# Attention inside a fused kernel: how the row sums are inverted and spread, and where the row maxima stand in VectorE's queue

## The chip, the cores and the metric

The kernel runs on one NeuronCore of a Trainium2 chip. The metric is the device time of one execution in microseconds (us); lower is better. PE is TensorE, DVE is VectorE, ACT is ScalarE, POOL is GpSimd and SP is the queue that issues the DMAs.

## The reference

```python
def _attn_ref(q, k, v):                      # 2 x 8 heads, 576 tokens, head dimension 64
    q_rot, k_rot = (rotate(q), rotate(k))    # rotary embedding
    scores = scale * np.matmul(q_rot, k_rot.transpose(0, 1, 3, 2))
    scores = scores - np.max(scores, axis=-1, keepdims=True)
    attn = np.exp(scores)
    attn = attn / (np.sum(attn, axis=-1, keepdims=True) + 1e-09)
    return np.matmul(attn, v).astype(np.float32)

def reference(**kwargs):
    attn_out = _attn_ref(**attn_kwargs)
    B, H, S, D = attn_out.shape
    x = np.ascontiguousarray(attn_out.transpose(0, 2, 1, 3)).reshape(B * S, H * D)
    x = _moe_ref(x=x, **moe_kwargs)          # x @ w_in, ELU, @ w_out (512 -> 2048 -> 512)
    return _moe2_ref(x=x, **moe2_kwargs)     # x @ w_in, Mish, @ w_out
```

## The kernel before

The kernel has two parts. Attention comes first, and behind it two feed-forward layers (ELU, then Mish). The change touches attention alone.

Attention works on pairs of heads, `NP` = 8 of them. A pair has nine tiles of 128 query rows: eight whole ones, and one that holds the last 64 rows of both heads (index 8). A tile is a step `u` of the loop in `attention()`; `i` is its index in the pair (`TPP` = 9) and `p` the pair. In a step the following instructions go to the engines' queues, each queue being worked off in the order in which it is written (`tc.manual_schedule()` leaves the order as it is in the program):

- `prepare`: GpSimd rotates the next but one pair (`rope_part`) and splits the next pair into high and low parts (`split_half`); SP issues the DMAs that stack these parts.
- `do_S(u)`: TensorE writes the scores of tile u to PSUM, in four matmuls of 288 columns (six for index 8). There are two score buffers, so `do_S(u)` needs the one that `do_exp(u - 2)` has read.
- `do_x`: VectorE multiplies a finished output group in `psA` by the inverse sums in `R`.
- `do_T(u - 3)` (`LAG` = 3): TensorE transposes the exponentials of the tile three steps back, into `psT` and `psL`.
- `do_inverse`, at i = 4 for the first four tiles of the pair (group g = 0) and at i = 0 of the next pair for the other five (g = 1): VectorE adds 1e-9 to the sums, takes the reciprocal, and copies each value 64 times into `rw` (for g = 1 it also multiplies a mask by the fifth column). Its first instruction waits for the sum that the exp of the step before leaves.
- `do_keep`: ScalarE copies the spread inverse sums from `psA` to `R`.
- `do_spread` and `do_av`, at the steps named in `plan`: TensorE turns the columns of `rw` into rows (a matmul with the identity), or multiplies the transposed exponentials `pt` with v, head by head, into 64 partitions of `psA` each. Spreads stand at i = 6 and i = 2, products with v at i = 7, 0, 3 and 5.
- `do_evac(u - 3)`: the transposed tile goes from `psT` to `pt`, on VectorE for the indices in `ON_DVE`, otherwise on ScalarE. `do_evac_last`, at three steps of a pair, takes `psL`, always on VectorE.
- `do_max(u)`: VectorE takes the extreme of each row of the scores (a minimum, since q was scaled by a negative number).
- `do_exp(u)`: ScalarE takes the exponential with that extreme as its bias, and leaves the row sum (`accum_out`).
- `do_xh` and `do_xl`, in the step after a group's last product: ScalarE rounds the output to its high part `XH`, and GpSimd subtracts that for the low part `XL` (VectorE in the last three pairs).
- From step 49 on, parts of the preparation of the first eight weight tiles (`weight_part`): one instruction on GpSimd, three on VectorE, one on ScalarE, one on GpSimd.

So the order on VectorE in a step was `do_x`, `do_inverse`, `do_evac`, `do_evac_last`, `do_max`; and the loop that sets the order of the work is do_S(u), do_max(u), do_exp(u), do_S(u + 2).

Of the kernel before, what the change touches and what calls it, by code (L numbers as in the profile page):

```python
# [10 lines left out]
F32 = mybir.dt.float32  # L11
F32R = mybir.dt.float32r
I32 = mybir.dt.int32
AF = mybir.ActivationFunctionType
ALU = mybir.AluOpType
AX = mybir.AxisListType
# [11 lines left out]
def kernel(  # L28
# [11 lines left out]
    nc = tc.nc  # L40
    NP = qk.shape[0]
# [12 lines left out]
    TPP = 9  # L54
    NU = NP * TPP
# [174 lines left out]
    def attention(att, ps, tail):  # L230
        idn = att.tile([128, 128], F32, name="idn")
        tab = att.tile([128, 4, S], F32, name="tab")
        idn2 = att.tile([128, 64], F32, name="idn2")
        half_mask = att.tile([128, 16], F32, name="half_mask")
        psT = [ps.tile([128, 4, 128], F32, name=f"psT{k}") for k in range(2)]
        psL = ps.tile([128, 4, 128], F32, name="psL")
        psA = ps.tile([128, 512], F32, name="psA")
# [97 lines left out]
        mn_t = {}  # L335
        sm_t = {}
        rc_t = {}
        R_t = {}
        ON_DVE = (0, 2, 4, 6)

        def do_S(u):
            p, i = divmod(u, TPP)
# [32 lines left out]
        def do_max(u):  # L375
            m = att.tile([128, 16], F32, tag="mn", name="mn", bufs=4)[:, 0:1]
            nc.vector.tensor_reduce(out=m, in_=psS[u][:, :, :HS], axis=AX.XY, op=ALU.min)  # L377
            mn_t[u] = m

        def do_exp(u):  # L380
            P = att.tile([128, S], F32, tag="P", name="P", bufs=PB)
            p, i = divmod(u, TPP)
            g, j = (0, i) if i < 4 else (1, i - 4)
            if j == 0:
                sm_t[p, g] = att.tile([128, 16], F32, tag="sm", name="sm", bufs=3)
            nc.scalar.activation(  # L386
                out=P.rearrange("p (j n) -> p j n", j=2), in_=psS.pop(u)[:, :, :HS],
                func=AF.Exp, scale=-1.0, bias=mn_t.pop(u), accum_out=sm_t[p, g][:, j:j + 1],
            )
            P_t[u] = P  # L390

        def do_inverse(p, g):
            n = 4 + g
            r = att.tile([128, 16], F32, tag="rc", name="rc", bufs=2)
            nc.vector.tensor_scalar(
                out=r[:, :n], in0=sm_t.pop((p, g))[:, :n], scalar1=1e-9, scalar2=None, op0=ALU.add
            )
            nc.vector.reciprocal(out=r[:, :n], in_=r[:, :n])
            w = att.tile([128, 3, 2, 64], F32, tag="rw", name="rw", bufs=1)
            nc.vector.tensor_copy(  # L400
                out=w[:, 0:2], in_=r[:, 0:4].rearrange("p (h t) -> p t h", h=2).unsqueeze(3).to_broadcast([128, 2, 2, 64])
            )
            if g:
                nc.vector.tensor_scalar(
                    out=w[:, 2], in0=half_mask[:, 0:2].unsqueeze(2).to_broadcast([128, 2, 64]),
                    scalar1=r[:, 4:5], scalar2=None, op0=ALU.mult,
                )
            rc_t[p, g] = w

        def do_spread(p, g):  # L410
            w = rc_t.pop((p, g))
            for t in range(2 + g):
                nc.tensor.matmul(
                    psA[:, 128 * t:min(128 * t + 128, 256 + 64 * g)],
                    lhsT=w[:, t].rearrange("p h d -> p (h d)"), rhs=idn if t < 2 else idn2,
                    start=True, stop=True,
                )

        def do_keep(p, g):
# [56 lines left out]
        def do_x(p, g):  # L476
            x = R_t[p, g]
            nc.vector.tensor_tensor(out=x, in0=psA[:, :(256, 320)[g]], in1=x, op=ALU.mult)
# [5 lines left out]
        def do_xl(p, g, eng):  # L484
            x, hi, lo = x_parts(p, g)
            eng.tensor_tensor(out=lo, in0=x, in1=plain(hi), op=ALU.subtract)
# [11 lines left out]
                pair.append(t)  # L498
            bd.append(pair)
        qb = [att.tile([128, 2, S], F32R, name=f"qb{i}") for i in range(2)]  # L500
        for r in range(2):
            rows = slice(64 * r, 64 * r + 64)
            nc.vector.memset(half_mask[rows, 0:1], 1.0 - r)
            nc.vector.memset(half_mask[rows, 1:2], float(r))
        split_alloc(0)
        def keep_warm(n):
            for _ in range(n):
# [40 lines left out]
        ends, spreads = {}, {}  # L548
# [6 lines left out]
        for u in range(max(av_at) + 2):  # L555
            p, i = divmod(u, TPP)
            for k in range(8):
                if i == (k if p else min(k + 2, 8)) and p + 1 < NP:
                    prepare(p + 1, k)
            if i == 8 and p + 1 < NP:  # L560
                load_v(p + 1)
            if p == NP - 3 and i == 1:
                open_job()
                open_job()
            if p == NP - 4 and i == 4:
                prefetch_weights(3)
            if u < NU:
                do_S(u)
            if u < LAG + 4:
                keep_warm(FILL[u])  # L570
            for (pp, g) in ends.get(u - 1, []):
                do_x(pp, g)
            if 0 <= u - LAG < NU:
                do_T(u - LAG)
            if i == 4 and u < NU:
                do_inverse(p, 0)
            if i == 0 and u:
                do_inverse(p - 1, 1)
            for (pp, g) in spreads.get(u - 1, []):
                do_keep(pp, g)  # L580
            for (pp, g, c) in av_at.get(u, []):
                if g == "r":
                    do_spread(pp, c)
                else:
                    do_av(pp, g, c)
            if u >= NU:
                tail(u - NU, False)
            if 0 <= u - LAG < NU:
                do_evac(u - LAG)
                if (u - LAG) % TPP in (3, 7, 8):  # L590
                    do_evac_last((u - LAG) % TPP)
            if u < NU:
                do_max(u)
                do_exp(u)
            if u == 0:
                for t in pt_t:
                    nc.vector.memset(t[S - 512:128, :, 4, :], 0.0)
                nc.vector.tensor_tensor(out=idn2, in0=idn[:, 0:64], in1=idn[:, 64:128], op=ALU.add)
            if u in (0, 2):
                nc.vector.memset(plain(qb[1 - u // 2][64:128]), 0.0)  # L600
            if u == 1:
                rope_half(1, 2, nc.vector)
                first_hi(*HEAD[-1])
                first_lo(*HEAD[-1])
                stack_q(0)
            for (pp, g) in ends.get(u - 1, []):
                do_xh(pp, g)
                do_xl(pp, g, nc.gpsimd if u < (NP - 3) * TPP else nc.vector)
            for _ in range(PARTS[u % 2] if u >= (NP - 3) * TPP + 4 else 0):
                if njob[0] < 2 * GF:  # L610
                    weight_part()
            if u >= NU:
                tmp_pool[0] = att
                tail(u - NU, True)
                tmp_pool[0] = None
# [262 lines left out]
```

## Time and profile before

| what | value |
|---|---|
| device time, median of 3 runs | 647.3 us (644.89 to 649.81) |
| the profiled execution | 651.54 us, its span 649.0 us |
| TensorE busy | 588.4 us (91%) |
| VectorE busy | 441.9 us (68%) |
| ScalarE busy | 354.8 us (55%) |
| GpSimd busy | 240.8 us (37%) |
| mean granted TensorE clock | 0.955 |

Attention takes the first third of the span: the first row maximum starts at 12.5 us, the last at 213.8 us. The pairs begin (by the maximum of their first tile) at 12.5, 43.0, 67.6, 89.7, 114.3, 138.8, 163.9 and 191.4 us. A share of busy time over the whole span mixes this part with the feed-forward part, so the views are read by stretches. A timeline row gives start, length, engine, line, instruction and tiles, and in brackets the idle time of the engine just before it with what ended that.

### The profile page before, as it was taken

To read this page: it belongs to the slowest core of one execution; us is meant where nothing else is said; L and a number is where in the kernel's file an instruction comes from. 1 tells how busy PE (TensorE), PEld (TensorE's weight loads), DVE (VectorE), ACT (ScalarE), POOL (GpSimd) and SP (SyncE) were. 2 spreads that over 40 slices of the span, in tenths; PEclk is the share of its full clock that TensorE was granted. 3 is DMA by queue.
4 is the path that set the end of the run, shared out by engine and by line. 5 is a ranking of instruction groups with operands and counts; after the bars stand their busy time and mean duration, and the time that the engine had idled before them with its cause. 6 is when DMAs were issued, how large, how long until landed. Compare 5 with 4: busy or idle time off the path is not lost.

```text
span 649.0 us, 10299 instructions
## 1 busy us (share of the span) xinstructions
PE 588.4 (91%) x3874; PEld 525.1 (81%) x3874; DVE 441.9 (68%) x679; ACT 354.8 (55%) x621; POOL 240.8 (37%) x218
## 2 busy tenths in 40 slices
PE   7888878778686879999999999999699999999997
PEld 6766656656454759999999999999489989989986
DVE  6656756666877247667777777879767966965552
ACT  2334444445345346665545455578477686485670
POOL 6576566482522102323232323244624524324000
PEclk9779989888799879999999999999989999999999
DMA  6572553751342101223222222313414223210022
GB/s 202 148 213 101 125 155 124 220 131 43 112 125 84 34 1 66 98 66 98 68 96 83 81 84 79 97 67 106 137 46 135 82 83 129 82 34 17 17 65 97
DMA packets 43921, 62.17 MB, mean 96 GB/s; under 512 B 13920, under 2 KB 32096, under 8 KB 43104
## 3 DMA queue, kind: packets, MB, share of 16 engines
q1 hardware_dynamic: 43872, 61.52, 31.3%
q8 instruction: 30, 0.49, 0.3%
q14 instruction: 19, 0.16, 0.1%
HBM read 46.20 MB, written 2.36 MB: 75 GB/s over the span
## 4 chain that ended last, share of the span: by engine, by line
PE 40%; issue 30%; DVE 13%; POOL 12%; ACT 5%; DMA 1%; SPq 0%; POOLq 0%; ACTq 0%; DVEq 0%
PE ps_h L709 15%; PE ps_s L183 12%; PE ps_s L370 5%; PE psA L463 4%; DVE mn L377 3%; POOL wu L96 3%; ACT P L386 3%; PE psT L431 3%; POOL wi1l L123 3%; POOL wo0l L123 2%; POOL wo1l L123 2%; POOL wi0l L123 2%; DVE wu L104 1%; DVE pt L445 1%; DVE rw L400 1%
## 5 line engine op out<-in xcount | busy, mean ns | idle before, releaser
L386 ACT ACTIVATE P<-ps_s,mn 128x576 f32<-128x576 f32 x72 | 53.3, 741 | 86.2 <-DVE mn L377 83.1
L463 PE MATMUL psA<-pt,v_t 128*64 128x256 f32 (+1 forms) x320 | 50.5, 450 | 22.5 <-ACT R L422 22.4
L377 DVE TENSOR_REDUCE mn<-ps_s 128x1 f32<-128x576 f32 x72 | 53.6, 745 | 17.0 <-PE ps_s L370 16.9
L123 POOL TENSOR_TENSOR wi1l<-wu,wi1h 128x512 fp32r<-128x512 f32 x16 | 25.3, 1579 | 101.6 <-ACT wi1h L122 101.6
L183 PE MATMUL ps_s<-XH,wi1h 128*128 128x288 f32 x256 | 54.5, 294 | 1.5 <-ACT tb L637 1.5
L183 PE MATMUL ps_s<-XH,wi0h 128*128 128x288 f32 x256 | 55.1, 297 | 0.8 <-DVE tb L218 0.7
L463 PEld LDWEIGHTS psA<-pt,v_t 128*64 128x64 f32 x320 | 21.6, 146 | 41.2 <-ACT R L422 25.9
L183 PE MATMUL ps_s<-XL,wi1h 128*128 128x288 f32 x256 | 54.7, 295 | 0.0
L183 PE MATMUL ps_s<-XL,wi0h 128*128 128x288 f32 x256 | 54.7, 295 | 0.0
L183 PE MATMUL ps_s<-XH,wi0l 128*128 128x288 f32 x256 | 54.5, 294 | 0.0
L183 PE MATMUL ps_s<-XH,wi1l 128*128 128x288 f32 x256 | 54.4, 293 | 0.0
L100 DVE TENSOR_SCALAR wu<-wu 128x512 int32<-128x512 int32 x64 | 31.3, 489 | 33.4 <-POOL wu L96 33.4
L104 DVE SCALAR_TENSOR_TENSOR wu<-raw,wu 128x512 int32<-128x512 int32 x64 | 49.6, 775 | 1.9
L370 PE MATMUL ps_s<-ka,qa 128*128 128x288 f32 x112 | 31.5, 365 | 20.1 <-ACT P L386 20.1
L108 DVE SCALAR_TENSOR_TENSOR wu<-raw,wu 128x512 int32<-128x512 int32 x64 | 48.0, 751 | 1.7
L123 POOL TENSOR_TENSOR wo0l<-wu,wo0h 128x512 fp32r<-128x512 f32 x16 | 25.3, 1583 | 64.2 <-ACT wo0h L122 60.7
L96 POOL TENSOR_SCALAR wu<-raw 128x512 f32<-128x512 f32 x64 | 47.2, 737 | 5.3
L431 PE MATMUL psT<-idn,P 128*128 128x128 f32 x288 | 47.9, 293 | 0.0
L123 POOL TENSOR_TENSOR wo1l<-wu,wo1h 128x512 fp32r<-128x512 f32 x16 | 24.2, 1515 | 62.1 <-ACT wo1h L122 62.1
L123 POOL TENSOR_TENSOR wi0l<-wu,wi0h 128x512 fp32r<-128x512 f32 x16 | 22.6, 1414 | 65.4 <-ACT wi0h L122 55.9
L217 DVE SCALAR_TENSOR_TENSOR tb<-ta,tb 128x576 f32<-128x576 f32 x30 | 22.7, 758 | 35.3 <-ACT tb L216 35.2
L370 PEld LDWEIGHTS ps_s<-ka,qa 128*128 128x128 f32 x112 | 18.3, 206 | 33.7 <-ACT P L386 25.3
(149 smaller groups left out, 1631.9 us busy)
## 6 DMA issues: line engine op xcount, KB each, us to landing
raw<-in_w_in_dram SPq DMA_DIRECT2D x32, 512.0 KB, 3.7
raw<-in_w_out_dram SPq DMA_DIRECT2D x32, 512.0 KB, 3.2
qk_t<-in_qk_dram SPq DMA_DIRECT2D x6, 1152.0 KB, 5.5
qa<-qh SPq DMA_DIRECT2D x28, 144.0 KB, 2.6
v_t<-in_vp_dram SPq DMA_DIRECT2D x8, 320.0 KB, 3.0
out_dram<-Y SPq DMA_DIRECT2D x9, 256.0 KB, 2.0
ka<-kh SPq DMA_DIRECT2D x14, 144.0 KB, 2.5
ka<-kl SPq DMA_DIRECT2D x14, 144.0 KB, 2.8
```

What stands on the lines that cost most here:

```text
L96: nc.gpsimd.tensor_scalar(out=u, in0=high.bitcast(F32), scalar1=REBASE, scalar2=0.0, op0=ALU.mult, op1=ALU.add)
L100: nc.vector.tensor_scalar(out=ui, in0=ui, scalar1=3, scalar2=0x7FFFFFF8, op0=ALU.logical_shift_left, op1=ALU.bitwise_and)
L104: nc.vector.scalar_tensor_tensor(out=ui, in0=high, scalar=-0x80000000, in1=ui, op0=ALU.bitwise_and, op1=ALU.bitwise_or)
L108: nc.vector.scalar_tensor_tensor(out=ui, in0=low, scalar=29, in1=ui, op0=ALU.logical_shift_right, op1=ALU.bitwise_or)
L123: nc.gpsimd.tensor_tensor(out=lo, in0=u, in1=plain(hi), op=ALU.subtract)
L183: nc.tensor.matmul(o[:, j, :HS], lhsT=w[:, cc, :], rhs=x[:, b, cc, j * HS:j * HS + HS], start=(k == 0), stop=(k == 3 * NC - 1),)
L370: nc.tensor.matmul(o[:, j, :HS], lhsT=l, rhs=r(slice(j * HS, j * HS + HS)), start=(a == 0), stop=(a == n - 1),)
L377: nc.vector.tensor_reduce(out=m, in_=psS[u][:, :, :HS], axis=AX.XY, op=ALU.min)
L386: nc.scalar.activation(out=P.rearrange("p (j n) -> p j n", j=2), in_=psS.pop(u)[:, :, :HS], func=AF.Exp, scale=-1.0, bias=mn_t.pop(u), acc ...
L431: nc.tensor.transpose(tv[:, c, :], P[:, c * 128:c * 128 + 128], idn)
L463: nc.tensor.matmul(o[64 * h:64 * h + 64, :n], lhsT=v_t[p][:, c, 64 * h:64 * h + 64], rhs=pt_t[g][:, h, c, :], start=(c == 0), stop=(c == 4),)
L709: nc.tensor.matmul(o, lhsT=l, rhs=w, start=(k == 0), stop=(k == 3 * GF - 1))
```

## The change

- The sums of a group go to every second element of one of three lasting tiles (`sums`), whose other elements are set to 1e-9 once. `do_inverse` adds the two elements of each pair (a reduction) and takes the reciprocal. The copy into `rw`, the mask and its multiplication are gone, and so are `half_mask` and `idn2`.
- `do_spread` takes the single column of inverse sums as stationary operand with a stride of zero, 64 times, for 64 partitions of `psA` at a time: four matmuls for g = 0 and six for g = 1, where there were two and three of 128 partitions.
- `do_max(u)` stands right behind `do_x`, ahead of `do_inverse` and of both evacuations.
- The evacuation of index 8 goes to VectorE and that of index 6 to ScalarE.
- `do_xh` and `do_xl` come one step later while the loop has score tiles left, and `do_xl` is on GpSimd for all pairs but the last.

```diff
@@ def attention
-        idn2 = att.tile([128, 64], F32, name="idn2")
-        half_mask = att.tile([128, 16], F32, name="half_mask")
+        sums = [att.tile([128, 8, 2], F32, name=f"sums{k}") for k in range(3)]
...
-        ON_DVE = (0, 2, 4, 6)
+        ON_DVE = (0, 2, 4, 8)
...
@@ def do_exp
-            if j == 0:
-                sm_t[p, g] = att.tile([128, 16], F32, tag="sm", name="sm", bufs=3)
+            sm_t[p, g] = sums[(2 * p + g) % 3]
             nc.scalar.activation(
                 out=P.rearrange("p (j n) -> p j n", j=2), in_=psS.pop(u)[:, :, :HS],
-                func=AF.Exp, scale=-1.0, bias=mn_t.pop(u), accum_out=sm_t[p, g][:, j:j + 1],
+                func=AF.Exp, scale=-1.0, bias=mn_t.pop(u), accum_out=sm_t[p, g][:, j, 0:1],
             )
@@ def do_inverse
             r = att.tile([128, 16], F32, tag="rc", name="rc", bufs=2)
-            nc.vector.tensor_scalar(
-                out=r[:, :n], in0=sm_t.pop((p, g))[:, :n], scalar1=1e-9, scalar2=None, op0=ALU.add
-            )
+            nc.vector.tensor_reduce(out=r[:, :n], in_=sm_t.pop((p, g))[:, :n, :], axis=AX.X, op=ALU.add)
             nc.vector.reciprocal(out=r[:, :n], in_=r[:, :n])
-            w = att.tile([128, 3, 2, 64], F32, tag="rw", name="rw", bufs=1)
-            nc.vector.tensor_copy(
-                out=w[:, 0:2], in_=r[:, 0:4].rearrange("p (h t) -> p t h", h=2).unsqueeze(3).to_broadcast([128, 2, 2, 64])
-            )
-            if g:
-                nc.vector.tensor_scalar(
-                    out=w[:, 2], in0=half_mask[:, 0:2].unsqueeze(2).to_broadcast([128, 2, 64]),
-                    scalar1=r[:, 4:5], scalar2=None, op0=ALU.mult,
-                )
-            rc_t[p, g] = w
+            rc_t[p, g] = r
@@ def do_spread
-            w = rc_t.pop((p, g))
-            for t in range(2 + g):
+            r = rc_t.pop((p, g))
+            for j in range(4):
+                h, t = divmod(j, 2)
                 nc.tensor.matmul(
-                    psA[:, 128 * t:min(128 * t + 128, 256 + 64 * g)],
-                    lhsT=w[:, t].rearrange("p h d -> p (h d)"), rhs=idn if t < 2 else idn2,
-                    start=True, stop=True,
+                    psA[64 * h:64 * h + 64, 128 * t:128 * t + 128],
+                    lhsT=r[:, j:j + 1].to_broadcast([128, 64]), rhs=idn, start=True, stop=True,
                 )
+            for h in range(2 * g):
+                nc.tensor.matmul(
+                    psA[64 * h:64 * h + 64, 256:320],
+                    lhsT=r[:, 4:5].to_broadcast([128, 64]), rhs=idn[:, 64 * h:64 * h + 64], start=True, stop=True,
+                )
@@ set-up
-        for r in range(2):
-            rows = slice(64 * r, 64 * r + 64)
-            nc.vector.memset(half_mask[rows, 0:1], 1.0 - r)
-            nc.vector.memset(half_mask[rows, 1:2], float(r))
+        for t in sums:
+            nc.vector.memset(t[:, :, 1:2], 1e-9)
@@ the loop over steps
             for (pp, g) in ends.get(u - 1, []):
                 do_x(pp, g)
+            if u < NU:
+                do_max(u)
             if 0 <= u - LAG < NU:
                 do_T(u - LAG)
...
             if u < NU:
-                do_max(u)
                 do_exp(u)
             if u == 0:
                 for t in pt_t:
                     nc.vector.memset(t[S - 512:128, :, 4, :], 0.0)
-                nc.vector.tensor_tensor(out=idn2, in0=idn[:, 0:64], in1=idn[:, 64:128], op=ALU.add)
...
-            for (pp, g) in ends.get(u - 1, []):
+            for (pp, g) in ends.get(u - (1 if u >= NU else 2), []):
                 do_xh(pp, g)
-                do_xl(pp, g, nc.gpsimd if u < (NP - 3) * TPP else nc.vector)
+                do_xl(pp, g, nc.gpsimd if pp < NP - 1 else nc.vector)
```

## Rows read from the trace of the kernel before

**Rows 1.** The page, part 2: granted TensorE clock, in tenths, in 40 slices
```profile
PEclk9779989888799879999999999999989999999999
```

**Rows 2.** Busy time by stretch; columns: stretch, length, engines, clock, DMA share, GB/s
```profile
12.00:43.00 31.00, 27.48 (x139) 21.73 (x139) 20.50 (x31) 9.74 (x24) 22.06 (x19) 0.72 0.59 162
...
67.60:89.70 22.10, 17.74 (x133) 13.61 (x133) 15.10 (x26) 11.40 (x27) 14.07 (x12) 1.00 0.49 139
89.70:114.30 24.60, 19.46 (x133) 15.15 (x133) 16.20 (x27) 11.39 (x27) 14.00 (x12) 0.93 0.43 122
...
138.80:163.90 25.10, 20.29 (x131) 16.23 (x132) 18.55 (x34) 12.45 (x29) 13.48 (x12) 0.86 0.33 89
163.90:191.40 27.50, 20.36 (x133) 14.75 (x132) 20.82 (x39) 12.64 (x30) 10.42 (x11) 0.88 0.45 126
191.40:213.80 22.40, 15.48 (x105) 11.49 (x104) 16.22 (x30) 11.65 (x27) 6.36 (x6) 0.96 0.27 86
...
236.00:649.00 413.00, 401.98 (x2687) 380.50 (x2685) 287.46 (x416) 250.62 (x383) 126.16 (x110) 0.99 0.25 79
```

**Rows 3.** Waits from 67.6 to 89.7; columns: us in total, times, longest us
```profile
ACT P L386 <- DVE mn L377: 7.7, 6, 4.1
POOL XL L486 <- ACT XH L482: 7.7, 2, 4.2
...
PE ps_s L370 <- ACT P L386: 2.4, 1, 2.4
...
PE psA L463 <- ACT R L422: 2.0, 2, 1.5
```

**Rows 4.** Timeline from 86 to 92, around the inverse sums of the second group
```profile
86.56 0.46 DVE L395 TENSOR_SCALAR rc<-sm 128x5 f32<-128x5 f32 x1 [0.96 <-ACT P L386]
...
87.71 1.51 DVE L404 TENSOR_SCALAR rw<-half_mask,rc 128x128 f32<-128x128 f32 x1
...
89.14 0.68 DVE L445 COPY pt<-psT 128x512 f32<-128x512 f32 x1
89.74 0.74 DVE L377 TENSOR_REDUCE mn<-ps_s 128x1 f32<-128x576 f32 x1
...
90.60 0.74 ACT L386 ACTIVATE P<-ps_s,mn 128x576 f32<-128x576 f32 x1 [4.07 <-DVE mn L377]
...
91.48 0.54 PE L370 MATMUL ps_s<-ka,qa 128*128 128x288 f32 x2 [2.40 <-ACT P L386]
```

**Rows 5.** Timeline of TensorE, 78 to 87: one step, a spread, products with v
```profile
78.33 0.53 PE L370 MATMUL ps_s<-ka,qa 128*128 128x288 f32 x2
78.70 0.43 PE L370 MATMUL ps_s<-ka,qb 128*128 128x288 f32 x2
...
79.50 0.61 PE L413 MATMUL psA<-idn,rw 128*128 128x128 f32 x4
79.87 0.51 PE L370 MATMUL ps_s<-ka,qa 128*128 128x288 f32 x2
...
82.66 1.08 PE L463 MATMUL psA<-pt,v_t 128*64 128x256 f32 x8 [1.47 <-ACT R L422]
...
86.30 1.06 PEld L463 LDWEIGHTS psA<-pt,v_t 128*64 128x64 f32 x12 [0.20 <-issue]
```

**Rows 6.** The tiles rc and rw: lengths in ns, shortest/median/longest; first and last start
```profile
L395 DVE TENSOR_SCALAR rc<-sm x16: 170/460/1218, 25.0 to 216.0; 128x4 f32<-128x4 f32 x8, 128x5 f32<-128x5 f32 x8
...
L400 DVE COPY rw<-rc x16: 293/501/1244, 25.4 to 216.5; 128x256 f32<-128x256 f32 x16
L404 DVE TENSOR_SCALAR rw<-half_mask,rc x8: 274/1511/1512, 41.0 to 216.7; 128x128 f32<-128x128 f32 x8
```

**Rows 7.** Timeline of VectorE, 12 to 25: the instruction that makes idn2
```profile
14.62 1.50 DVE L598 TENSOR_TENSOR idn<-idn 128x64 f32<-128x64 f32 x1
```

**Rows 8.** The tile XL, written from attention: lengths in ns, shortest/median/longest
```profile
L486 POOL TENSOR_TENSOR XL<-R,XH x8: 724/798/867, 46.7 to 131.5; 128x256 fp32r<-128x256 f32 x4, 128x320 fp32r<-128x320 f32 x4
L486 DVE TENSOR_TENSOR XL<-R,XH x8: 424/492/1522, 142.4 to 236.6; 128x256 fp32r<-128x256 f32 x4, 128x320 fp32r<-128x320 f32 x4
```

More of the change, by code (lines that the diff above doesn't have):

```diff
@@ L394, in do_inverse, with do_spread @@
             r = att.tile([128, 16], F32, tag="rc", name="rc", bufs=2)
-            nc.vector.tensor_scalar(
-                out=r[:, :n], in0=sm_t.pop((p, g))[:, :n], scalar1=1e-9, scalar2=None, op0=ALU.add
-            )
+            nc.vector.tensor_reduce(out=r[:, :n], in_=sm_t.pop((p, g))[:, :n, :], axis=AX.X, op=ALU.add)
             nc.vector.reciprocal(out=r[:, :n], in_=r[:, :n])
-            w = att.tile([128, 3, 2, 64], F32, tag="rw", name="rw", bufs=1)
-            nc.vector.tensor_copy(
-                out=w[:, 0:2], in_=r[:, 0:4].rearrange("p (h t) -> p t h", h=2).unsqueeze(3).to_broadcast([128, 2, 2, 64])
-            )
-            if g:
-                nc.vector.tensor_scalar(
-                    out=w[:, 2], in0=half_mask[:, 0:2].unsqueeze(2).to_broadcast([128, 2, 64]),
-                    scalar1=r[:, 4:5], scalar2=None, op0=ALU.mult,
-                )
-            rc_t[p, g] = w
-        def do_spread(p, g):
-            w = rc_t.pop((p, g))
-            for t in range(2 + g):
+            rc_t[p, g] = r
+        def do_spread(p, g):
+            r = rc_t.pop((p, g))
[4 more added lines that the diff above has]
+                    lhsT=r[:, j:j + 1].to_broadcast([128, 64]), rhs=idn, start=True, stop=True,
+                )
+            for h in range(2 * g):
                 nc.tensor.matmul(
-                    psA[:, 128 * t:min(128 * t + 128, 256 + 64 * g)],
-                    lhsT=w[:, t].rearrange("p h d -> p (h d)"), rhs=idn if t < 2 else idn2,
-                    start=True, stop=True,
+                    psA[64 * h:64 * h + 64, 256:320],
+                    lhsT=r[:, 4:5].to_broadcast([128, 64]), rhs=idn[:, 64 * h:64 * h + 64], start=True, stop=True,
                 )
```

## Prediction

> **What bounds the kernel now.** I read the clock by slices first, then the busy time by stretches cut at the pairs' first maxima, then the waits of one undisturbed pair, and last its timeline around the inverse sums.
>
> The feed-forward part is TensorE's: 402.0 of its 413.0 us are busy [rows 2]. Nothing in the diff touches it, so what attention gives back reaches the end in full. In attention TensorE is not full. The pair from 67.6 to 89.7, all of it at the full clock (1.00, that is 2.4 GHz), lasts 22.1 us with 17.74 us of matmul, so 4.4 us are idle; the other engines have less to do (DVE 15.1, POOL 14.1, ACT 11.4) [rows 2]. The waits name the 4.4: 2.4 us in one piece for a score buffer (PE ps_s <- ACT P) and 2.0 us for the kept inverse sums (PE psA <- ACT R) [rows 3]. Behind both stands ScalarE waiting for maxima, 7.7 us [rows 3].
>
> The 2.4 can be followed. VectorE reaches the inverse sums at 86.56, has them spread out in SBUF after 89.1, then evacuates (89.14), and only then takes the maximum (89.74) whose scores were long there; the exp follows at 90.60 after 4.07 us of idle ScalarE, and the next scores at 91.48 [rows 4]. The maximum stands last in VectorE's step, behind instructions that wait for things which it doesn't need.
>
> Seven of the first thirteen slices show a clock under 9 tenths [rows 1]. In the next pair it is 0.93, part of it at 1.2 GHz: the same 133 matmuls take 19.46 instead of 17.74 us and the pair 24.6 [rows 2]. The four pairs from 43.0 to 138.8 take 95.8 us; three of them look like this one. The 2.4 us gap preceded that drop [rows 4], but the pair at 67.6 had such a gap too and kept its clock [rows 2, 3].
>
> **The change part by part.**
>
> *Maxima ahead.* Count the loop by its rows. Scores take 78.33 to 79.13, 0.8 us [rows 5]; from the maximum's start to the next scores in that buffer it is 89.74 to 91.48, 1.74 us [rows 4]; together some 2.6 us for two steps. TensorE's own work for two steps of scores and transposes is 2 x 1.17 us (78.33 to 79.87 less the 0.37 of the spread [rows 5]), 2.3 us, and any two neighbouring steps also hold a product with v (eight records take 1.08 us) or a spread [rows 5]. So with the maximum first, TensorE is the slower of the two nearly everywhere. What comes late instead is the evacuation, by one maximum (0.74 us [rows 4]). Its reader, a product with v, comes a step or more later, and the transposes that need the psT buffer two steps later, so TensorE's 2.3 us cover it; without this cover 0.74 us on each VectorE evacuation would be lost. I leave 0.4 us of idle per pair for the steps in which VectorE has a whole evacuation, the psL evacuation and a maximum one after the other. The 2.0 us for the kept sums go by the same cause: ScalarE's keep is queued behind an exp that waited for its maximum. The later do_xh also leaves that queue clear ahead of the first group's keep (it now stands ahead of the second group's instead, 0.4 us, one step after its spread was written).
>
> *Inverse sums.* The reduction in place of the addition: nearest is that addition, 0.17 to 1.22 us, median 0.46 [rows 6]; I take 0.2, near its short end: its long ones, like the copy's (0.29 to 1.24), are the same work stretched, and the reduction that there is, the maximum, is not stretched in these rows (0.74 us [rows 4]). The reciprocal stays. Gone are the copy (0.29 to 1.24) twice a pair and the masked product (0.27, mostly 1.51) once [rows 6]. That is 2 x 0.5 + 1.5 = 2.5 us of VectorE per pair, on the path at i = 0 only, where the first part already counts the gap; so no second gain for it, but it is what lets the evacuation behind it be in time.
>
> *Spread.* Four records of 128 columns take 0.37 us (79.50 to 79.87), 0.093 each [rows 5]; a record is one pass, and each matmul has two. There will be 8 records for g = 0 and 12 for g = 1 (four of them with 64 columns), in place of 4 and 6. In the products with v, eight records of 256 columns take 1.08 us, 0.135 each [rows 5], so the two 64-partition halves overlap. With such overlap a spread rises by some 0.15 us, without by 0.4. Going into the 64-wide form, the load port stood 0.20 us idle with nothing to wait for [rows 5]; in and out that is up to 0.4 more. Per pair: +0.3 to +1.6; I take 0.8, since the order h, h, other h, other h lets only neighbours overlap.
>
> The Trainium skill, TensorEngine Tiling (Array Packing), Overview to Key Properties, speaks against this step: changing the tiling mode drains TensorE, although tiles of one mode run in parallel. The trace agrees with the second half by the 1.08 us; the 0.20 us is the only row that bears on the first. By that rule at the upper price the sum below would lose 6 us.
>
> *Evacuation of index 8 to VectorE, of 6 to ScalarE.* One for one, 0.68 us either way [rows 4]; with index 8 VectorE has nothing else that waits, so zero, at worst 0.1 per pair.
>
> *Low parts.* Six of the eight that VectorE did (median 0.49 us) go to GpSimd (0.80) [rows 8]. In the stretches concerned GpSimd is busy 13.5 of 25.1, 10.4 of 27.5 and 6.4 of 22.4 us [rows 2], which covers 0.8 us each; without the cover 5 us. GpSimd waits 7.7 us per pair for the high parts [rows 3]; these come a step later, but one rotation more is now queued ahead of them, and the splits and their stacking DMAs queued behind are needed only in the next pair.
>
> The Trainium skill, GPSIMD Engine Reference, section 4.1, also advises against it: a two-input elementwise operation is about twice as slow there. Here it is 1.6 times by the medians; if GpSimd were the path this would cost 2 us.
>
> *Set-up.* idn2 goes: 1.50 us at 14.62, ahead of the second maximum [rows 7].
>
> **The sum.** A pair becomes 17.74 + 0.8 + 0.4 = 18.9 us.
> - 43.0 to 138.8: 4 x 18.9 = 75.6 instead of 95.8: -20.2.
> - 138.8 to 191.4, two pairs with weight work: 52.6 now. VectorE falls from 20.8 to about 17.5 (2.5 less, and the low parts), close to TensorE's 18.5; idle beyond that of an early pair is now up to 7.1 - 4.4 = 2.7 us [rows 2]. I leave 1.6 of it: 2 x 20.5 = 41.0: -11.6.
> - 191.4 to 213.8: 18.9 instead of 22.4: -3.5.
> - 12 to 43: one gap of the 2.4 kind and part of the 1.5: -3. The clock is 0.72 there and TensorE busy for 27.5 of 31.0 [rows 2], so not more.
> - Two of the seven pairs keep a stretch at 1.2 GHz, 1.7 us each: +3.4.
>
> Together -35: a span of 614 from 649.0, and 616.5 from the profiled 651.5. That execution was 4.2 above the median of the runs shown, 647.3; from the median it is 612.
>
> **The rivals.**
> - *TensorE takes back what it is given.* Spreads at the upper price (+0.8 in 7 or 8 pairs, 6 us), a stretch at 1.2 GHz in each pair (5 x 1.7 = 8.5 us) and weight pairs at 21.6 (2 us): -18, so 629. For it: such a stretch stands in nearly every pair now. Against: 18.5 of 18.9 us busy is far above today's 80%. 620 to 632: 0.16.
> - *ScalarE takes VectorE's place.* In steps with its evacuation, the exp waits for transposes and evacuation. If that leaves 0.5 us in three places of each pair, 12 us are lost: 624. 0.08.
> - *GpSimd's order.* 14.07 busy and 7.7 waiting fill 21.8 of its 22.1 us [rows 2, 3]. If the waits stay, four pairs take 22.1 (-7.4) and the rest gains some 7: 633. Against: it waits because it is ahead; what it prepares is read a pair later. 0.06.
> - *The stride of zero, the case that ends slower.* No row has a weight load that reads one element 64 times. There are 64 + 96 = 160 such records; at 0.135 us each they fit the sum, and from 0.135 + 35/160 = 0.35 us each they eat all of the gain. At 0.45 us it is 663. Against: the load moves as many elements as now. 0.04.
>
> **How the numbers follow.** The forecast, 601 to 620, gets 0.66. Its lower end has the spread at +0.3 (-3.8), idle at 0.2 per pair (-1.5), no stretch at 1.2 GHz (-3.4) and weight pairs at 19.5 (-2): -46. The range 601 to 629 takes in the second rival whole and most of the first, and leaves out some 0.15. About 1% is what a measurement of this kernel can tell from no change, 6.5 us: all but the last rival and an accident lie below 640.8. Faster 0.93, same 0.03, slower 0.04.
>
> **What would show it.** In the profile after: pairs of about 19 us, nearly equal from 40 to 110; TensorE busy for 18 us or more of each; ACT P <- DVE mn much below 7.7 us a pair; the maximum right behind its scores; a spread of 0.5 to 0.9 us; the clock at 9 tenths in the slices of attention; the feed-forward part 413 us as now. Wrong it would be if VectorE's inverse or GpSimd's low parts held up something that I took as covered, or if a spread took over 2 us.

## The result and the profile after

The changed kernel takes 600.85 us (median of 4 runs, 598.55 to 602.46) against 648.55 us for the kernel before: a ratio of 0.926 with a 95% interval of 0.920 to 0.933, 7.4% faster. The forecast was 612 us, its range 601 to 629: right in direction and in mechanism, too small in size, and the time lies just under the range. The profiled execution took 600.88 us with a span of 599.1; 649.0 before, so 49.9 us less in the span. Of three kernels tried below (runs 8, 11 and 13) one execution each was in a slower state of the chip, and is left out of their medians.

Busy time of the changed kernel by stretch, cut at the pairs' first maxima as in [rows 2]; columns as there (stretch, length, PE, PEld, DVE, ACT, POOL, clock, DMA share, GB/s):

```profile
12.00:35.60 23.60, 21.64 (x121) 17.39 (x121) 16.90 (x25) 10.16 (x24) 16.49 (x14) 0.79 0.52 130
35.60:55.30 19.70, 19.70 (x146) 14.40 (x145) 11.95 (x23) 10.61 (x26) 16.69 (x16) 0.92 0.71 225
55.30:73.30 18.00, 18.00 (x145) 13.53 (x144) 11.90 (x23) 11.06 (x28) 14.03 (x12) 1.00 0.59 171
...
109.30:129.90 20.60, 18.84 (x152) 13.95 (x152) 16.80 (x28) 12.05 (x29) 17.12 (x15) 1.00 0.45 119
129.90:151.20 21.30, 18.39 (x147) 13.64 (x145) 19.96 (x33) 13.59 (x34) 15.91 (x15) 1.00 0.60 165
151.20:170.10 18.90, 16.66 (x132) 11.99 (x129) 16.88 (x30) 11.33 (x27) 8.46 (x9) 1.00 0.39 125
...
186.10:599.10 413.00, 402.97 (x2692) 381.96 (x2688) 290.68 (x419) 251.24 (x384) 125.67 (x110) 0.99 0.25 79
```

The reader is to see the third row: an early pair has no TensorE idle left, 18.00 busy of 18.00 us, where [rows 2] had 17.74 of 22.10. Two more pairs repeat it to the hundredth. The feed-forward part is 413 us as before (from its first matmul behind the last products with v it is 413.5 before and 412.7 now), so all but some 1 us of the gain is in front of it.

The waits of that early pair (us in total, times, longest), to be read against [rows 3]:

```profile
DVE mn L376 <- PE ps_s L369: 4.3, 8, 1.3
POOL XL L478 <- ACT XH L474: 3.7, 2, 2.6
...
ACT P L384 <- DVE mn L376: 1.7, 4, 0.7
PEld ps_s L369 <- ACT P L384: 0.9, 2, 0.5
```

The direction has turned: ScalarE waits 1.7 us for maxima instead of 7.7, and the maximum now waits for TensorE's scores, 4.3 us. The timeline around the second group's inverse, against [rows 4]:

```profile
73.08 0.73 ACT L384 ACTIVATE P<-ps_s,mn 128x576 f32<-128x576 f32 x1
73.29 0.76 DVE L376 TENSOR_REDUCE mn<-ps_s 128x1 f32<-128x576 f32 x1 [0.32 <-PE ps_s L369]
...
73.97 0.15 DVE L393 TENSOR_REDUCE rc<-sums 128x5 f32<-128x10 f32 x1
74.16 0.19 DVE L394 RECIPROCAL rc<-rc 128x5 f32<-128x5 f32 x1
74.27 0.75 ACT L384 ACTIVATE P<-ps_s,mn 128x576 f32<-128x576 f32 x1
```

From the end of the scores (73.29) to the exp (74.27) it is 1 us now, and the inverse stands behind the maximum without holding anyone: it is done in 0.4 us.

Clock by slices, against [rows 1]:

```profile
PEclk8789999999999999999999999998899999999999
```

After the third slice, attention runs at the full clock; the last stretch at 1.2 GHz in it ends at 38.8 us, in the second pair.

### The profile page after: what moved, and what is told of

Same layout as the page of the kernel before. It is cut to its first block, busy times and chain, and to the rows that moved or that the text cites. A ratio compares the mean times of both kernels' runs of the same rounds, so it can differ in the third digit from the quotient of the medians.

```text
span 599.1 us, 10450 instructions
## 1 busy us (share of the span) xinstructions
PE 573.2 (96%) x3954; PEld 511.9 (85%) x3954; DVE 420.5 (70%) x647; ACT 353.0 (59%) x621; POOL 247.9 (41%) x224
## 4 chain that ended last, share of the span: by engine, by line
PE 42%; issue 30%; POOL 13%; DVE 7%; DMA 4%; SPq 1%; ACT 1%; POOLq 0%; ACTq 0%; DVEq 0%
PE ps_h L699 16%; PE ps_s L183 13%; PE psA L455 4%; PE ps_s L369 4%; POOL wu L96 4%; POOL wi1l L123 3%; PE psT L423 3%; POOL wo0l L123 2%; DMA qk_t<-in_qk_dram 2%; POOL wo1l L123 2%; POOL wi0l L123 2%; DVE mn L376 2%; DVE wu L104 1%; DMA ka<-kh 1%; DVE wu L100 1%
## 5 line engine op out<-in xcount | busy, mean ns | idle before, releaser
L104 DVE SCALAR_TENSOR_TENSOR wu<-raw,wu 128x512 int32<-128x512 int32 x64 | 51.6, 806 | 1.9
L96 POOL TENSOR_SCALAR wu<-raw 128x512 f32<-128x512 f32 x64 | 49.5, 774 | 5.2
L455 PE MATMUL psA<-pt,v_t 128*64 128x256 f32 (+1 forms) x320 | 46.8, 424 | 4.9 <-ACT R L414 4.9
L108 DVE SCALAR_TENSOR_TENSOR wu<-raw,wu 128x512 int32<-128x512 int32 x64 | 49.6, 774 | 1.7
L439 ACT ACTIVATE pt<-psT 128x512 f32<-128x512 f32 x40 | 23.9, 597 | 42.2 <-PE psT L423 42.2
L123 POOL TENSOR_TENSOR wo0l<-wu,wo0h 128x512 fp32r<-128x512 f32 x16 | 23.7, 1480 | 54.4 <-ACT wo0h L122 54.4
L217 DVE SCALAR_TENSOR_TENSOR tb<-ta,tb 128x576 f32<-128x576 f32 x30 | 22.8, 758 | 33.4 <-ACT tb L216 33.2
L183 PEld LDWEIGHTS ps_s<-XH,wi1h 128*128 128x128 f32 x256 | 41.9, 191 | 4.1 <-ACT tb L627 3.5
L214 ACT ACTIVATE tb<-ps_s 128x576 f32<-128x576 f32 x30 | 19.6, 652 | 42.4 <-PE ps_s L183 42.4
L626 ACT ACTIVATE ta<-ps_s 128x576 f32<-128x576 f32 x32 | 20.6, 643 | 39.7 <-PE ps_s L183 39.7
L423 PE MATMUL psT<-idn,P 128*128 128x128 f32 x288 | 43.8, 275 | 0.0
```

What stands on the lines that cost most here:

```text
L96: nc.gpsimd.tensor_scalar(out=u, in0=high.bitcast(F32), scalar1=REBASE, scalar2=0.0, op0=ALU.mult, op1=ALU.add)
L104: nc.vector.scalar_tensor_tensor(out=ui, in0=high, scalar=-0x80000000, in1=ui, op0=ALU.bitwise_and, op1=ALU.bitwise_or)
L108: nc.vector.scalar_tensor_tensor(out=ui, in0=low, scalar=29, in1=ui, op0=ALU.logical_shift_right, op1=ALU.bitwise_or)
L123: nc.gpsimd.tensor_tensor(out=lo, in0=u, in1=plain(hi), op=ALU.subtract)
L183: nc.tensor.matmul(o[:, j, :HS], lhsT=w[:, cc, :], rhs=x[:, b, cc, j * HS:j * HS + HS], start=(k == 0), stop=(k == 3 * NC - 1),)
L423: nc.tensor.transpose(tv[:, c, :], P[:, c * 128:c * 128 + 128], idn)
```

## The experiments

An "early pair" is one of the second to the fifth at the full clock: 22.1 us before, 18.0 after. Its length and the other lengths below are differences of the maxima's starts in the timeline.

**1. The maximum first, alone.** In the kernel before:

```diff
                 do_x(pp, g)
+            if u < NU:
+                do_max(u)
             if 0 <= u - LAG < NU:
...
             if u < NU:
-                do_max(u)
                 do_exp(u)
```

> The kernel before with one edit: the maximum stands ahead of the inverse, the transposes' evacuation and the psL evacuation in VectorE's queue. Theory A, that of the prediction (the place of the maximum carries the gain, the length of the inverse has no gain of its own): 30 us or more of the 48 us are gained, 618 us or less, and ScalarE's wait for maxima in an early pair falls from 7.7 to under 3 us. Theory B (two causes of the same size that need each other: what the first frees is stopped again by the second, an inverse of up to 2.7 us in front of the evacuations): only 10 to 20 us are gained, 628 to 638 us, and TensorE stays idle for 2 us or more of an early pair.

624.9 us, ratio 0.960 (0.955 to 0.965). An early pair takes 19.9 us, ScalarE's wait 3.8 us. That lies between the two theories, nearer to the second: about half of the gain. What is left idle is named by the waits of such a pair:

```profile
PEld psL L432 <- DVE pt L457: 1.2, 1, 1.2
PEld psA L463 <- ACT R L422: 1.1, 2, 0.7
```

The long inverse stands in front of the psL evacuation in VectorE's queue, and the next transposes into psL wait for its one buffer. So the inverse has a price of its own once the maximum is out of its way.

**2. The short inverse, alone.** In the kernel before, the parts of the diff in `do_exp`, `do_inverse`, `do_spread`, `sums` and idn2; the order of the loop, the engines of the evacuations and the place of the high and low parts as before.

> The kernel before with the short inverse (two-element sum, reciprocal, spread from a stride-zero column, no idn2) alone; the maximum stays last. Theory A: the gap at the second group's inverse shrinks by what is taken out of it, 2 to 2.5 us a pair, and no more: 8 x 2.3 plus the 1.5 us of idn2, about 20 us, 628 us, with some 2.5 us of TensorE idle left in each early pair. Theory B: the same 10 to 20 us. Theory C (the inverse is the cause, the order hardly matters): 35 us or more, 613 us or less.

631.9 us, ratio 0.972 (0.967 to 0.977). An early pair takes 20.3 us. It is what A and B have in common; C is out. The single gains, 22.1 to 19.9 and to 20.3, are 2.2 and 1.8 us; their sum, 4.0, is about what the whole change gains, 4.1. (No run holds these two edits and nothing else.)

**3. The maximum back, in the changed kernel.** The first edit reversed.

> The changed kernel with the maximum back at its old place, behind the evacuations. Theory A: it loses 25 us or more, 625 us or above. Theory B: it loses 10 to 20 us, 611 to 621 us, TensorE idle for about 2 us of an early pair again. Theory C: it loses under 10 us.

616.9 us, ratio 0.948 (0.942 to 0.954), an early pair 20.2 us: 16 us lost, as theory B has it.

**4. The old inverse, in the changed kernel.** The second edit reversed.

> The changed kernel with the old inverse (addition, reciprocal, copy, masked product, spreads of 128 partitions) and idn2. Theory A: it loses at most 6 us, since the inverse now stands behind the maximum and is covered: 607 us or less. Theory B: it loses 8 to 20 us, 609 to 621 us, early pairs of about 19 us instead of 18.0, with TensorE waiting for an evacuation behind the inverse. Theory C: it loses over 25 us.

610.5 us, ratio 0.938 (0.933 to 0.944), an early pair 19.0 us: 9.6 us lost, as theory B has it. The wait for psL (PEld psL <- DVE pt, 1.2 us) is back in it. Of the two, the order is the larger part and the shorter inverse the smaller, and neither covers the other.

The rest of the change (index 8 for index 6, the high and low parts a step later, the low parts on GpSimd) is not small beside one of them alone: run 4 holds it beside the maximum and is 14.4 us faster than run 1, run 3 holds it beside the inverse and is 15.0 us faster than run 2, most of both in the last three pairs and behind the last maximum. Which of its parts does that was not tried; taken singly out of the changed kernel they are worth less (runs 5 to 7).

**5. Index 8 and index 6 back.** In the changed kernel:

```diff
-        ON_DVE = (0, 2, 4, 8)
+        ON_DVE = (0, 2, 4, 6)
```

> The changed kernel with the evacuation of index 8 back on ScalarE and that of index 6 on VectorE. Theory A (the prediction: one for one, at most 0.1 us a pair): within 1 us of the changed kernel's 601 us. Theory B (the index-8 evacuation is the first thing that the next pair, and the end of attention, wait for on ScalarE, ahead of an exp or a keep): 2 to 5 us slower, half of it after the last maximum, where the wait for the kept sums goes from 2.65 back towards 4.55 us.

607.0 us, ratio 0.934 (0.929 to 0.940), 6.2 us more than the changed kernel, whose interval (0.920 to 0.933) it still touches; early pairs 18.05 us, unchanged. Theory A, the prediction's, is right by the pairs and wrong by the end of attention, where theory B has the place: from the last maximum to the first feed-forward matmul that follows the last products with v it is 19.5 us, 16.3 in the changed kernel. The wait there:

```profile
PE psA L455 <- ACT R L414: 4.5, 1, 4.5
```

It is 2.65 us in the changed kernel. Not all of the 3.2 us is this wait, though. The last products with v, in the kernel before, the changed kernel, run 5, run 11 and run 10 (the changed kernel once more):

```profile
229.94 5.60 PE L463 MATMUL psA<-pt,v_t 128*64 128x320 f32 x20 [4.55 <-ACT R L422]
...
183.57 2.91 PE L455 MATMUL psA<-pt,v_t 128*64 128x320 f32 x20 [2.65 <-ACT R L414]
...
188.40 4.34 PE L455 MATMUL psA<-pt,v_t 128*64 128x320 f32 x20 [4.46 <-ACT R L414]
...
223.07 4.60 PE L463 MATMUL psA<-pt,v_t 128*64 128x320 f32 x20 [2.74 <-ACT R L422]
...
183.09 4.38 PE L455 MATMUL psA<-pt,v_t 128*64 128x320 f32 x20 [2.65 <-ACT R L414]
```

The wait goes with the edit, 4.5 us without and 2.7 with it, a difference of 1.8. The length of the products goes with a stretch at 1.2 GHz that falls on them or not: in run 10 the unchanged kernel takes 4.38 us for them and 17.8 us in place of 16.3. So 1.8 of the 3.2 us are the edit's and 1.4 the clock's.

ScalarE before, at the end of attention:

```profile
224.70 0.60 ACT L447 ACTIVATE pt<-psT 128x512 f32<-128x512 f32 x1 [2.84 <-PE psT L431]
225.19 0.65 ACT L214 ACTIVATE P<-ps_s 128x576 f32<-128x576 f32 x1
...
229.47 0.42 ACT L422 ACTIVATE R<-psA 128x320 f32<-128x320 f32 x1
```

and after:

```profile
177.21 0.64 ACT L214 ACTIVATE P<-ps_s 128x576 f32<-128x576 f32 x1
...
183.10 0.42 ACT L414 ACTIVATE R<-psA 128x320 f32<-128x320 f32 x1
```

Before, the ELU of the first feed-forward tile stood behind the last tile's evacuation, which waited for its transposes; the keep stands behind that ELU, and the last products with v behind the keep. With the evacuation on VectorE the ELU starts while TensorE still transposes: the last transposes start at 179.51, the ELU at 177.21. The rest of the 6.2 us is in the other stretches, in part at 1.2 GHz (the last but one pair 22.9 us), and I can't put it down to this edit: the second profile of the unchanged kernel (run 10) has 22.8 there too.

**6. Low parts back to VectorE, 7. high and low parts one step earlier.** In the changed kernel, one each:

```diff
-                do_xl(pp, g, nc.gpsimd if pp < NP - 1 else nc.vector)
+                do_xl(pp, g, nc.gpsimd if u < (NP - 3) * TPP else nc.vector)
```
```diff
-            for (pp, g) in ends.get(u - (1 if u >= NU else 2), []):
+            for (pp, g) in ends.get(u - 1, []):
```

> The changed kernel with the low parts of the later pairs on VectorE again (as before, one step later). Theory A (the prediction: the engine of the low parts is worth nothing by itself): within 1 us of 601 us. Theory B (in the weight pairs VectorE is what the rest waits for, and each low part there also waits for ScalarE's high part with maxima queued behind): the two pairs of 20.6 and 21.3 us become 1 us longer each, 603 to 606 us.

603.4 us, ratio 0.930 (0.924 to 0.935). The last three pairs take 62.9 us instead of 60.8, but the first of them has a stretch at 1.2 GHz (its mean clock is 0.93) that the changed kernel's profile has not, and the two pairs of theory B do not both grow (22.8 and 20.3 for 20.6 and 21.3 us). The interval overlaps with that of the changed kernel: not decided.

> The changed kernel with high and low parts one step earlier, as before. Theory A (ScalarE has room, only the place beside a keep counts): early pairs stay within 0.3 us of 18.0 and the time within 2 us of 601. Theory B (the high part in front of the first group's keep delays the product with v, as it did before): 0.4 us per pair, 3 to 4 us slower.

600.4 us, ratio 0.926 (0.920 to 0.932), early pairs 18.13 us: theory A; the later step makes no difference that can be measured.

**8. Every spread twice.** In the changed kernel:

```diff
+            for _ in range(2):
-            for j in range(4):
+                for j in range(4):
...
-            for h in range(2 * g):
+                for h in range(2 * g):
```

> The changed kernel with every spread's matmuls issued twice, 160 more records (nothing else changes). Theory A (early pairs are TensorE's alone, 18.0 busy of 18.0, and a stride-zero load costs what any load of 64 columns costs): each early pair grows by the issue time of the records, 8 x 0.06 and 12 x 0.06, 1.1 us, to 19.1 us, and the time by 6 to 9 us. Theory B (TensorE looks busy only because records overlap, another engine sets the 18.0): pairs stay within 0.3 us of 18.0.

607.0 us, ratio 0.935 (0.929 to 0.941). A profile of the same kernel was taken in a later run:

> The same kernel as the run with doubled spreads, for a profile at the usual speed of the chip. Theory A (TensorE alone sets the early pairs): pairs of 19.1 us, TensorE busy all of them. Theory B (another engine sets them): 18.0 to 18.3 us.

607.0 us, early pairs 19.07 us. One of them, by stretch:

```profile
54.70:73.80 19.10, 19.10 (x166) 14.63 (x165) 11.95 (x23) 11.13 (x28) 14.10 (x13) 1.00 0.56 161
```

Theory A: twenty more records cost 1.05 us, 0.053 each, and nothing hides them. TensorE alone sets the early pairs. And 0.053 us for 128 columns (64 in four of the twenty) is little more than half of the 0.093 that a 128-wide record took before [rows 5]. The single records in this trace show how: the first eight of a spread start in twos, at 59.10 and 59.12, 59.21 and 59.23, 59.32 and 59.34, with 0.11 us from one two to the next, and 0.11 us is also what lies between two of the 128-wide transposes near by (57.22, 57.33, 57.44), which start one by one. So two 64-wide passes go in the time of one, and the stride of zero costs nothing. The load and the passes of the spread in the changed kernel (ns, shortest/median/longest):

```profile
L401 PEld LDWEIGHTS psA<-idn,rc x128: 132/136/138, 27.8 to 180.4; 128*64 128x64 f32 x128
L401 PE MATMUL psA<-idn,rc x128: 272/273/324, 27.8 to 180.5; 128*64 128x128 f32 x128
...
L393 DVE TENSOR_REDUCE rc<-sums x16: 146/151/165, 24.5 to 171.8; 128x4 f32<-128x8 f32 x8, 128x5 f32<-128x10 f32 x8
```

**9. Weight work earlier and even.** In the changed kernel:

```diff
-        PARTS = (1, 2)
+        PARTS = (1, 1)
...
-            if p == NP - 3 and i == 1:
+            if p == NP - 4 and i == 1:
...
-            if p == NP - 4 and i == 4:
+            if p == NP - 5 and i == 4:
...
-            for _ in range(PARTS[u % 2] if u >= (NP - 3) * TPP + 4 else 0):
+            for _ in range(PARTS[u % 2] if u >= (NP - 4) * TPP + 4 else 0):
```

> The changed kernel with the preparation of the first eight weight tiles begun one pair earlier and at an even pace of one part a step (32 parts in 32 steps, from step 40). Theory A (in the weight pairs VectorE's bursts of two parts in front of a maximum cost the 2.6 and 3.3 us above 18.0): these pairs come down to 18.5 to 19.5 us, the pair ahead of them grows to at most 18.7, and the time falls by 2 to 4 us to 597 to 599. Theory B (the work as such costs it, through GpSimd, which has 14.0 busy of 18.0 us in an early pair): the excess moves one pair forward, 600 to 603 us.

613.5 us, ratio 0.944 (0.941 to 0.948): slower than the changed kernel, by neither theory. One pair, from 108.3 to 138.8, takes 30.4 us. SP's queue there, and the wait that it made:

```profile
112.98 0.33 SPq L83 DMA_DIRECT2D raw<-in_w_out_dram  x1
113.41 0.38 SPq L261 DMA_DIRECT2D v_t<-in_vp_dram  x1
121.33 0.33 SPq L83 DMA_DIRECT2D raw<-in_w_out_dram  x1
121.70 0.42 SPq L256 DMA_DIRECT2D qk_t<-in_qk_dram  x1
```
```profile
POOL qk_t L269 <- DMA qk_t<-in_qk_dram: 13.7, 1, 13.7
```

The last pair's queries and keys are queued behind a weight load that waits for one of three buffers until VectorE is through with an older tile.

**10. The changed kernel again**, for a second profile.

> The changed kernel once more, for a second profile. If the start (first pair at its end at 35.6 us, where the forecast had 40) and the clock of attention are the kernel's own, this profile repeats them within 1 us and shows 18.0 us pairs; if the place of the stretches at 1.2 GHz is chance, the end of the first pair moves by 1 to 3 us with them while the 18.0 us stay.

603.0 us; the first pair ends at 35.3 us, early pairs 18.02 us. The stretches at 1.2 GHz lie elsewhere (the second pair is at the full clock now, 18.0 us instead of 19.6). The second pair's length moves with them. Whether the end of the first pair does, these two profiles can't tell, since in both the clock is full from 21.7 to 35.3; run 5's profile has 1.2 GHz from 24.1 to 37.7, and its first pair ends at 38.6.

**11. Index 8 alone**, the reverse of edit 5, in the kernel before.

> The kernel before with one edit: index 8 evacuated on VectorE and index 6 on ScalarE. Theory A (it matters only where attention ends, ScalarE's elu starting before the last tile's evacuation instead of behind it): from the last maximum to the first feed-forward matmul behind the last products with v 4 to 5 us less, pairs as before, 643 to 645 us. Theory B (it matters in each pair, since VectorE's index-6 evacuation stands in front of a maximum too): 1 us a pair more, 636 us. Theory C (only worth something once TensorE is the bound): within 1 us of before.

639.1 us, ratio 0.984 (0.978 to 0.989). Early pairs as before (22.1, or 23.9 with a stretch at 1.2 GHz); from the last maximum to the feed-forward matmuls 18.6 instead of 21.6 us, 1.8 of it the wait and 1.0 the clock of the last products with v (the rows of run 5). Theory A in the place. The time is better than that place explains; the rest lies in the start and in other pairs, part of it by their clock, and no run takes it apart.

**12. idn2 put back** in the changed kernel, after the memsets of step 0:

```diff
+                nc.vector.tensor_tensor(out=idn2, in0=idn[:, 0:64], in1=idn[:, 64:128], op=ALU.add)
```

> The changed kernel with the instruction that made idn2 put back in its old place (nothing reads the result). Theory A (the prediction: it stands on VectorE ahead of the second maximum and on the path): the end of the first pair moves from 35.5 to about 37 us and the time by 1.5 us. Theory B (the start of attention waits for the second pair's stacked operands, which come by DMA, so there is slack on VectorE): the first pair ends within 0.5 us of 35.5 and the time stays at 601 to 602 us.

601.3 us, ratio 0.925 (0.922 to 0.929): no share in the time that stands out of the noise, as B has it. The first pair ends at 36.9, as A has it, but idn2 need not be the reason. The stretch from 12 to 35 in the changed kernel, run 1 (which has idn2), this run and run 5 (which has not), the third column from the right being the clock:

```profile
12.00:35.00 23.00, 21.04 (x118) 16.79 (x117) 16.90 (x25) 10.16 (x24) 15.89 (x14) 0.79 0.51 128
...
12.00:35.00 23.00, 20.13 (x119) 16.15 (x119) 16.85 (x27) 9.56 (x23) 15.88 (x14) 0.85 0.53 136
...
12.00:35.00 23.00, 20.78 (x103) 15.83 (x103) 15.39 (x24) 8.32 (x20) 15.85 (x14) 0.70 0.52 132
...
12.00:35.00 23.00, 20.34 (x99) 15.50 (x99) 15.67 (x22) 8.32 (x20) 16.31 (x14) 0.69 0.52 135
```

Their first pairs end at 35.6, 34.6, 36.9 and 38.6: the end goes with the clock, with idn2 or without.

**13. Weight work earlier, without a load that waits.** Edit 9, and inside attention at most two weight loads ahead:

```diff
-        prefetch_weights(3)
+        prefetch_weights(3 if late_pool[0] is not None else 2)
```

> The kernel with the weight preparation one pair earlier at one part a step, now with at most two weight loads ahead inside attention, so that no load on SP waits for a buffer. Theory A (bursts of two VectorE parts in front of a maximum cost the excess): the pairs with weight work take 18.3 to 19.3 us, the last pair's load is in time, and the time is 595 to 598 us, below the changed kernel's 601. Theory B (the work as such, on VectorE and GpSimd, costs it): the excess is the same in sum, spread over three pairs, 600 to 603 us.

597.8 us, ratio 0.922 (0.917 to 0.926): no clear gain over the changed kernel's 0.926 (0.920 to 0.933). The last three pairs take 21.7, 18.6 and 16.8 us instead of 20.6, 21.3 and 18.9 (the last is counted to its ninth maximum). The first of them is GpSimd's:

```profile
125.00:146.60 21.60, 19.84 (x152) 14.04 (x152) 19.09 (x31) 12.28 (x30) 21.19 (x19) 1.00 0.58 154
```

21.2 of 21.6 us busy. That the other two pairs are shorter fits theory A, and GpSimd takes back some of it (theory B). But these two pairs also hold fewer parts, 9 each where the changed kernel has 13 and 11, so the bursts are not shown apart from the amount.

## Why the prediction came out too high

The mechanism was right for the early pairs: TensorE waited for ScalarE, ScalarE for a maximum that stood behind work it didn't need; with the order changed TensorE is the bound of these pairs (run 8), and attention's gain reaches the end of the kernel. What the prediction named to be seen in the profile is there: nearly equal pairs, the wait of 7.7 us down to 1.7, a spread of 0.6 us, the full clock from the third pair on, 413 us behind attention. Its case that ends slower, the stride of zero, is out by run 8. In the early pairs neither ScalarE nor GpSimd took VectorE's place, since TensorE sets them.

What failed are terms of the sum, -35 forecast against -49.9 in the profiled spans:

| term | forecast | measured | off by |
|---|---|---|---|
| four pairs after the first, at the full clock | -20.2 | -23.7 | -3.5 |
| two pairs with weight work | -11.6 | -10.7 | +0.9 |
| the last pair, to its last maximum | -3.5 | -3.5 | 0 |
| the first pair | -3 | -7.4 | -4.4 |
| stretches at 1.2 GHz kept | +3.4 | +1.6 | -1.8 |
| behind the last maximum | 0 | -6.2 | -6.2 |

- *"One for one ... so zero"*, the evacuation of index 8, is the step that failed, and with it the sum, which left out the stretch behind the last maximum. I priced the instruction and not its place in ScalarE's queue at the end of attention. Runs 5 and 11 show 1.8 us for it, the wait for the kept sums (4.55 us before, 2.65 after). Another 2.7 of the 6.2 us are the clock: the last products with v take 2.91 us at the full clock where they took 5.60 in a stretch at 1.2 GHz, and run 10 (4.38 us) shows that this differs between executions of one kernel. The last 1.6 us lie in small pieces, half of them in the feed-forward part.
- *"TensorE busy for 27.5 of 31.0, so not more"*, the first pair. An engine that is busy at 0.72 of the clock is not a full one; the same work at a higher clock is shorter. Run 5, at the clock of before (0.69 from 12 to 35 in both), ends its first pair at 38.6 instead of 43.0, 4.5 us earlier; the other 3 of the 7.4 us are the clock, which run 5 and run 12 did not get back. The cut has a part in the 7.4 too. Before, the maximum that ends the stretch came 4.9 us after its scores had begun, now it comes 1.7 us after, and 18 fewer records of TensorE fall into the stretch (121 for 139). Cut at these scores, the gain is 4.3 us, and the rest shows in the stretches behind. Their rows before and after:

```profile
38.16 0.51 PE L370 MATMUL ps_s<-ka,qa 128*128 128x288 f32 x2
...
33.89 0.50 PE L369 MATMUL ps_s<-ka,qa 128*128 128x288 f32 x2 [1.17 <-DMA qb<-ql]
```

  What these scores wait for now is the second pair's stacked operands, which come by DMA. No run shows the 1.50 us of idn2 that I put on the path (runs 1 and 12).
- *The 1.2 GHz allowance.* I left it for two of seven pairs; the first profile has one, up to 38.8 us in the second pair (19.6 instead of 18.0 us). Run 10 has one in a weight pair and one behind the last maximum. That TensorE's idle gaps were what brought the drops is what the profiles suggest, kernel by kernel; I did not try it by itself.
- *The pair's 18.9 us.* Both additions were too large: the spread costs 0.3 a pair instead of 0.8 (18.00 busy less 17.74), and no idle is left where I kept 0.4. I had argued that the order of its matmuls lets only neighbours overlap; the records of run 8 overlap in all of a spread. The rule of the Trainium skill that I held against the step, TensorEngine Tiling (Array Packing), Key Properties (a change of tiling mode drains TensorE), agrees with the trace in the 0.20 us of issue ahead of a spread; with the overlap within the mode, stated on the same list, both together come to no more than these 0.3 us a pair.

```profile
68.17 0.42 PEld L401 LDWEIGHTS psA<-idn,rc 128*64 128x64 f32 x8 [0.20 <-issue]
```

- *"So no second gain for it"*, the shorter inverse. It has one, 1.8 us a pair alone and 1.0 us behind the other edits (19.0 to 18.0, run 4), since psL's evacuation stands behind it. In the sum this hid, because I took TensorE's work as the floor.
- *The last pair.* That it fits is luck: I put the 18.9 us of a whole early pair for it, nine steps without weight work, while the stretch is counted to the ninth maximum, eight steps, with weight work in them.
- *The weight pairs.* VectorE was to fall from 20.8 to about 17.5 us; it is 16.80 in the first and 19.96 in the second.
- *Low parts.* Zero was forecast; run 6 gives 2.5 us, not clear of noise. Whether the Trainium skill's advice in GPSIMD Engine Reference, section 4.1, counts here (VectorE for elementwise work, since GpSimd is about twice as slow with two inputs) stays open: VectorE is the fuller engine in the second weight pair (19.96 of 21.3 us, GpSimd 15.91), GpSimd in the first (17.12 of 20.6 us, VectorE 16.80).

What stays open: how much of the 49.9 us is the clock. A bound can be read off. Attention's stretch before and after:

```profile
12.00:236.00 224.00, 177.53 (x1144) 136.46 (x1145) 148.32 (x247) 100.42 (x233) 108.95 (x95) 0.89 0.41 117
...
12.00:186.10 174.10, 162.58 (x1223) 122.92 (x1222) 124.49 (x214) 98.45 (x232) 117.24 (x101) 0.96 0.52 151
```

At mean clocks of 0.89 and 0.96 they lack 24.6 and 7.0 us of full clock, so by this estimate at most some 18 us of the gain are the clock; eight pairs at the 4.1 us that an early one gains at the full clock would be 33. Runs of one kernel differ by some 4 us, with the mean clock going along (0.988 at 598.6 us, 0.983 at 602.5), and no experiment here sets it. Open is also what the rest of the change does in the last three pairs (runs 3 and 4 against 2 and 1). The time lies 0.15 us under the range, and two executions of the same kernel lie inside it (602.5 and 603.0 us): that it fell just outside is chance, the terms above are not.

## What to carry to other kernels

In an in-order queue, put the instruction that another engine's chain waits for ahead of those whose readers come later; two causes in one queue add up, so undo each of them alone before calling one the cause. When an engine's instruction is moved, price it at the end of the loop too, where other work is queued behind it. A busy share at half the clock says little about how much there is to gain.

## What was not expected of the hardware

- A stationary operand read with a stride of zero loads in 136 ns for 64 columns, as an ordinary one does (137 in the products with v), and two 64-wide passes of 128 columns overlap to 0.053 us each (run 8).
- The two-element reduction takes 0.15 us in every place (146 to 165 ns), also while GpSimd runs; the addition that it replaces took 0.17 to 1.22 us [rows 6].
- Weight instructions of VectorE stretch beside GpSimd's: one form took 0.69 us at 149.30 in the kernel before, where GpSimd ran nothing from 147 to 152, and 1.78 us here, with the GpSimd instructions around it in the second fence:

```profile
119.51 1.78 DVE L104 SCALAR_TENSOR_TENSOR wu<-raw,wu 128x512 int32<-128x512 int32 x1
```
```profile
119.14 1.60 POOL L269 TENSOR_TENSOR qk_t<-qk_t,tab 128x576 f32<-128x576 f32 x1
120.70 1.87 POOL L271 TENSOR_TENSOR qk_t<-qk_t,tab 128x576 f32<-128x576 f32 x1
```
